# Tanh-shrink feed-forward on one core: opening and steps 0 to 8 written as one list, later weight conversions dealt over other steps

## The chip, the core and the metric

One core of a Trainium2 chip runs the whole program as one launch. The metric is the device time of that launch in microseconds; lower is better. The engines have names here as in the profile: PE (TensorE), DVE (VectorE), ACT (ScalarE), POOL (GpSimd), SP (the queue that issues the DMAs).

## What is computed

Three stages in a row on 2176 tokens of width 512: banded attention with global tokens, a soft mixture of experts with 32 slots, and a feed-forward with a tanh-shrink. Only the end of the second stage and the third matter here:

```python
    return (c @ slot_out).astype(np.float32)   # end of _moe_ref, c is the softmax over 32 slots
...
def _moe2_ref(x, w_in, w_out) -> np.ndarray:
    h = x @ w_in
    g = h - np.tanh(h)
    return (g @ w_out).astype(np.float32)
```

w_in is 512 x 2048 and w_out 2048 x 512, both in float64 in memory.

## The kernel before

**What the feed-forward does.** The kernel never forms x. It folds the slot outputs into w_in: M = slot_out @ w_in has 32 rows, and h = c @ M. M is made in five blocks of columns (`BLOCKS`: 128, 384 and three of 512). The 17 tiles of 128 tokens are worked in six phases (`PHASES`) of 6, 6 and 5 tiles, each for eight of the 16 chunks of 128 hidden columns; that gives 48 steps, steps 0 to 15 and 24 to 39 with six tiles, 16 to 23 and 40 to 47 with five. The PE accumulates one phase's tiles in six PSUM banks, tile a. At the end of a phase of the first half (steps 7, 15, 23) ACT copies each bank to SBUF (`keep_part`, L1220), and the next phase's first products reuse the bank.

**One step i.** For each of its two parts (three and three tiles, or three and two): the head `g_head`, one product on the PE into a PSUM tile h (L1171; two banks in rotation); `g_square` on ACT (L1178); `g_tail0` and `g_tail1` on DVE (L1184, L1188), which make g = h³(h² - 2.5) (the factor -2/15 stands at the output); `g_hi` on ACT rounds g to the PE's short form (L1195) and `g_lo` on POOL takes the remainder (L1199). `ff` then issues three products of 512 columns for each tile: hi with the weight's hi (L1212), hi with its lo (L1213), lo with its hi (L1214). So a six-tile step has 18 products and two heads. The loop works two steps ahead: in step i the PE does the products of step i and the heads of i + 2 and i + 3, and the tails belong to step i + 2.

**Conversions.** Each chunk of w_out (c = 0 to 15) and of the later half of w_in (c = 24 to 31) must become float32 first. One conversion is an ACT operation on the raw words (`f32_head`, L542), then three on DVE: `shift` (L546, tensor_scalar), `high` (L551) and `low` (L556, both with two SBUF inputs). For w_out come two more: the weight's hi on ACT (L1072) and its lo on POOL (L1073). They go through two buffers k_w. The table `JOBS` gives the step in which a chunk is converted, `MB` the steps in which the fourth and fifth block of M are made. In the step's program order on DVE: first tail, second tail, S (shift), first tail, H (high), second tail, L (low).

**The order.** The scheduler is off (`tc.manual_schedule`); each engine runs its instructions in the order in which the code issues them. The opening, from L1276 to the loop at L1370, is straight code: conversion 0, the sums over slots scaled and turned (sos, sot, soT), blocks 0 to 2 of M (`m_rows` L1121, `m_rows_out` L1130, `m_parts` L1135, `m_hi` L1139, `m_lo` L1143), the heads and tails of steps 0 to 2 and the products of step 0. The loop takes over with step 1.

## Time and profile before

| | us |
|---|---|
| median of 3 runs | 403.71 (402.14 to 404.92) |
| the profiled execution | 403.34 |
| its span in the trace | 401.5 |
| PE busy | 380.0 (95%) |
| DVE busy | 275.1 (69%) |
| ACT busy | 218.2 (54%) |
| POOL busy | 208.5 (52%) |

The feed-forward's share begins at about 173 us of the span, behind the last product of the experts, and lasts to the end. The granted clock of the PE is full (1.00) in every stretch from 172 us to 390 us. A profile's busy time of the PE counts overlapping products with modelled ends; how fast it goes is read from the distance between starts.

### The profile page before, as it was taken

To read this page: it belongs to the slowest core of one execution; us is meant where nothing else is said; L and a number is where in the kernel's file an instruction comes from. 1 tells how busy PE (TensorE), PEld (TensorE's weight loads), DVE (VectorE), ACT (ScalarE), POOL (GpSimd) and SP (SyncE) were. 2 spreads that over 40 slices of the span, in tenths; PEclk is the share of its full clock that TensorE was granted. 3 is DMA by queue.
4 is the path that set the end of the run, shared out by engine and by line. 5 is a ranking of instruction groups with operands and counts; after the bars stand their busy time and mean duration, and the time that the engine had idled before them with its cause. 6 is when DMAs were issued, how large, how long until landed. Compare 5 with 4: busy or idle time off the path is not lost.

```text
span 401.5 us, 10209 instructions
## 1 busy us (share of the span) xinstructions
PE 380.0 (95%) x3767; PEld 281.3 (70%) x3767; DVE 275.1 (69%) x833; ACT 218.2 (54%) x542; POOL 208.5 (52%) x275
## 2 busy tenths in 40 slices
PE   6979989898999899999999999999989999999994
PEld 3768777677888333337877786886868888888873
DVE  3577787776576346359998786697879997555541
ACT  2677876765786103258656645565675554445430
POOL 2667685574673010018866433555565667447441
PEclk8999999999999899999999999999999999999999
DMA  7799999999879999997112101013000003003004
GB/s 181 206 398 322 353 327 306 347 349 306 297 214 291 331 360 418 417 419 284 55 33 73 52 1 54 0 23 122 15 2 2 0 26 132 0 2 123 36 2 139
DMA packets 33978, 70.43 MB, mean 175 GB/s; under 512 B 3840, under 2 KB 10752, under 8 KB 33920
## 3 DMA queue, kind: packets, MB, share of 16 engines
q1 hardware_dynamic: 33776, 69.56, 50.8%
q8 instruction: 32, 0.52, 0.5%
q14 instruction: 26, 0.21, 0.2%
q10 hardware_dynamic: 144, 0.13, 0.1%
HBM read 65.22 MB, written 4.46 MB: 174 GB/s over the span
## 4 chain that ended last, share of the span: by engine, by line
PE 77%; issue 6%; DVE 5%; POOL 5%; ACT 4%; DMA 1%; SPq 0%; DVEq 0%; POOLq 0%; ACTq 0%
PE a L1214 13%; PE a L1212 13%; PE a L1213 13%; PE sc L248 7%; PE a L1007 4%; PE X L281 4%; PE a L1046 4%; PE h L1171 3%; PE ptp L269 3%; PE gsc L441 2%; POOL slot L1199 2%; PE xTp L317 2%; DVE slot L1188 1%; PE xgp L486 1%; POOL q L210 1%
## 5 line engine op out<-in xcount | busy, mean ns | idle before, releaser
L1199 POOL TENSOR_TENSOR slot<-slot 128x384 fp32r<-128x384 f32 x96 | 98.6, 1031 | 83.5 <-ACT slot L1195 81.6
L1212 PE MATMUL a<-slot 128*128 128x512 f32 x272 | 107.1, 394 | 1.3 <-ACT v_w L1220 0.7
L1214 PE MATMUL a<-slot 128*128 128x512 f32 x272 | 107.7, 396 | 0.0
L1213 PE MATMUL a<-slot 128*128 128x512 f32 x272 | 107.3, 394 | 0.0
L1184 DVE SCALAR_TENSOR_TENSOR h<-slot,h 128x384 f32<-128x384 f32 x96 | 51.6, 537 | 39.4 <-ACT slot L1178 39.1
L1195 ACT CAST slot<-slot 128x384 fp32r<-128x384 f32 x96 | 47.7, 497 | 49.0 <-DVE slot L1188 48.5
L1178 ACT ACTIVATE slot<-h 128x384 f32<-128x384 f32 x96 | 45.4, 474 | 34.7 <-PE h L1171 34.2
L1212 PEld LDWEIGHTS a<-slot 128*128 128x128 f32 x272 | 51.1, 188 | 13.9 <-ACT v_w L1220 1.5
L1214 PEld LDWEIGHTS a<-slot 128*128 128x128 f32 x272 | 51.0, 188 | 11.5
L1213 PEld LDWEIGHTS a<-slot 128*128 128x128 f32 x272 | 51.1, 188 | 9.2 <-POOL slot L1073 1.1
L1188 DVE TENSOR_TENSOR slot<-slot,h 128x384 f32<-128x384 f32 x96 | 50.8, 530 | 7.3
L258 ACT ACTIVATE sm<-sm,mb 128x128 f32<-128x128 f32 x128 | 41.3, 397 | 17.4 <-DVE mb L254 17.1
L248 PE MATMUL sc<-k,q 128*64 128x128 f32 x512 | 40.3, 299 | 5.1 <-ACT q L216 2.6
L210 POOL TENSOR_SCALAR v<-v 32x1300 f32<-32x1300 f32 (+5 forms) x40 | 33.3, 833 | 15.9 <-PE xgp L486 12.8
L248 PEld LDWEIGHTS sc<-k,q 128*64 128x64 f32 x512 | 34.2, 208 | 9.3 <-issue 5.4
L210 POOL TENSOR_SCALAR q<-q 64x256 f32<-64x256 f32 x62 | 27.7, 447 | 19.2 <-issue 7.7
L1073 POOL TENSOR_TENSOR slot<-k_w,slot 128x512 fp32r<-128x512 f32 x16 | 20.8, 1297 | 31.8 <-ACT slot L1072 31.8
L254 DVE CUSTOM_DVE_ANT_0 sm<-sc,mask 128x128 f32<-128x128 f32 x128 | 29.9, 284 | 5.1 <-PE sc L248 4.6
L1171 PE MATMUL h<-slot 128*128 128x384 f32 x96 | 32.5, 341 | 0.9 <-DVE slot L1188 0.6
L1171 PEld LDWEIGHTS h<-slot 128*128 128x128 f32 x96 | 17.9, 187 | 12.1 <-DVE slot L1188 5.9
L281 PE MATMUL X<-v,pt 128*32 128x65 f32 x1024 | 23.4, 223 | 2.3 <-issue 2.2
L281 PEld LDWEIGHTS X<-v,pt 128*32 128x32 f32 x1024 | 17.1, 109 | 8.4 <-issue 7.4
(245 smaller groups left out, 528.2 us busy)
## 6 DMA issues: line engine op xcount, KB each, us to landing
slot<-in_w_dram SPq DMA_DIRECT2D x54, 512.0 KB, 7.3
slot<-in_w_out_dram SPq DMA_DIRECT2D x9, 512.0 KB, 3.7
slot<-in_w_in_dram SPq DMA_DIRECT2D x16, 256.0 KB, 6.9
k<-in_k_dram SPq DMA_DIRECT2D x7, 576.0 KB, 7.5
q<-in_q_dram SPq DMA_DIRECT2D x15, 256.0 KB, 5.4
out_dram<-o SPq DMA_DIRECT2D x15, 256.0 KB, 2.2
slot<-in_w_in_dram SPq DMA_DIRECT2D x7, 512.0 KB, 9.8
v<-in_v_dram SPq DMA_DIRECT2D x8, 390.0 KB, 5.1
```

Of the source, the lines that this page charges most:

```text
L210: G.tensor_scalar(out=o, in0=i, scalar1=0.0, scalar2=1.0, op0=ALU.add, op1=ALU.mult)
L248: T.matmul(sc[64 * i:64 * i + 64, a, :], lhsT=q_b[2][:, 256 * i + jj:256 * i + 256:4], rhs=k[:, i, :, WINDOWS[t][jj][0]], skip_group_check ...
L281: T.matmul(X[32 * jj:32 * jj + 32, h, :], lhsT=pt[:, 128 * jj + 32 * h:128 * jj + 32 * h + 32], rhs=v[:, WINDOWS[t][jj][0], 65 * h:65 * h ...
L1171: T.matmul(h, lhsT=mst(128 * fc, 128), rhs=cst(128 * t0 + c.start, n))
L1178: S.activation(out=u, in_=h, func=AF.Square)
L1184: V.scalar_tensor_tensor(out=h, in0=u, scalar=-2.5, in1=h, op0=ALU.add, op1=ALU.mult)
L1188: V.tensor_tensor(out=g, in0=u, in1=h, op=ALU.mult)
L1195: S.copy(out=ghi, in_=g)
L1199: G.tensor_tensor(out=glo, in0=g, in1=ghi.bitcast(F32), op=ALU.subtract)
L1212: T.matmul(acc_t[j], lhsT=ghi[:, c], rhs=whi[fc], start=first, stop=False)
L1213: T.matmul(acc_t[j], lhsT=ghi[:, c], rhs=wlo[fc], start=False, stop=False)
L1214: T.matmul(acc_t[j], lhsT=glo[:, c], rhs=whi[fc], start=False, stop=last)
```

## The change

**One list.** The straight code of the opening and the loop's steps 1 to 8 are replaced by `OPENING`, a string of 274 words; each word is one operation with its step, part or chunk (`t0:5:1` is the first tail of step 5, part 1; `T:2:3` the three products of tile 3 of step 2; `S:4`, `H:4`, `L:4` the DVE operations of chunk 4, `head:4` its ACT operation; `h`, `sq`, `hi`, `lo` as above; `keep:2` the copy of bank 2). The loop starts at step 9. With the list come four edits of the opening: the scaling of the sums is cut into an ACT half and a DVE half; the turn multiplies by a four-fold selector (`irep_m`), so that its result can be used by block 0 of M as an ordinary product of full width, which needs no copy and no second product; block 1's copy goes to DVE; part 0 of step 0 is cut into 128 and 256 columns (parts 2 and 3). The two products that only kept the PE busy (`keep_warm`, 512 and 256 columns) become one of 256.

**The later conversions.** Chunk 28 moves from step 13 to 12, 30 and 31 from 16 and 17 to 15 and 16, chunks 8, 9 and 10 from 19, 20, 22 to 18, 19, 21, chunk 12 from 25 to 24; block 3 of M from step 13 to 14. `AHEAD`, which paces the loads, goes from 5 to 4.

```diff
-EARLY, AHEAD = 8, 5
+EARLY, AHEAD = 8, 4
 JOBS = {
-    1: 3, 2: 4, 3: 5, 4: 6, 5: 7, 7: 24, 8: 25, 10: 26, 11: 27, 13: 28, 14: 29, 16: 30, 17: 31,
-    19: 8, 20: 9, 22: 10, 23: 11, 25: 12, 26: 13, 28: 14, 29: 15,
+    1: 3, 2: 4, 3: 5, 4: 6, 5: 7, 7: 24, 8: 25, 10: 26, 11: 27, 12: 28, 14: 29, 15: 30, 16: 31,
+    18: 8, 19: 9, 21: 10, 23: 11, 24: 12, 26: 13, 28: 14, 29: 15,
 }
-MB = {13: 3, 19: 4}
+MB = {14: 3, 19: 4}
+OPENING = """
+    sos:0 sos:1 head:1 S:1 turn:0 turn:1 turn:2 turn:3 soT:0 m0:0 m0:1 soT:1 m0:2 m0:3 head:2 mhi:0 H:1 L:1 whi:1
+    wlo:1 mlo:0 rows:1 ms:1 S:2 h:0:2 sq:0:2 h:0:3 sq:0:3 h:0:1 sq:0:1 t0:0:2 t1:0:2 t0:0:3 t1:0:3 hi:0:2 parts:1
...
+"""
+LOOP = 9
...
+        def sums_copy(k):
+            c = slice(256 * k, 256 * k + 256)
+            if k:
+                V.tensor_scalar(out=sos[:, c], in0=sop[:, c], scalar1=rr, scalar2=None, op0=ALU.mult)
+            else:
+                S.activation(out=sos[:, c], in_=sop[:, c], func=AF.Copy, scale=rr)
...
+        def m_first(k):
+            if k == 0:
+                mp_t[0] = bank(0)[:, 0:128]
+            T.matmul(mp_t[0], lhsT=soT[:, k, :], rhs=win[k][:, 0:128], start=k == 0, stop=k == 3)
...
+        for word in OPENING.split():
+            name, *a = word.split(":")
+            ops[name](*map(int, a))
...
         for i, (t0, nt, fc, first, last) in enumerate(steps):
-            while late and len(free) + len(cool) > 1 and len(LATE) - len(late) < 3 + sum(k < i + AHEAD for k in JOBS):
-                load_late()
-            if i == 0:
+            if i < LOOP:
                 continue
+            late_loads(i)
```

The PE behind the last product of the experts, before: turn (L1289), rows of blocks 0, 1, 2 (L1121), second products (L1135) and the first heads (L1171).

```order
L1289 MATMUL h<-istk,sos 128x32 x4
L1121 MATMUL a_3203<-win_100,mask_93 32x128 x4
L1121 MATMUL a_3208<-win_100,mask_93 32x384 x4
L1121 MATMUL a_3216<-win_101,mask_93 32x512 x4
L1135 MATMUL a_3222<-ms,mask_94 128x128
L1135 MATMUL a_3227<-ms,mask_94 128x384
L1171 MATMUL h<-slot 128x384 x2
L1135 MATMUL a_3244<-ms,mask_94 128x512
L1171 MATMUL h<-slot 128x384
L654 MATMUL a_3252<-win_100,ident 128x256
```

The same place after the change; L1327 is block 0's product of full width, L1355 are the heads of 128 and 256 columns.

```order
L1318 MATMUL h<-mask_94,sos 128x128 x4
L1327 MATMUL a_3207<-win_100,soT 128x128 x4
L1139 MATMUL a_3220<-win_100,soT 32x384 x4
L1355 MATMUL h<-slot 128x128
L1355 MATMUL h<-slot 128x256
L1196 MATMUL h<-slot 128x384
L1153 MATMUL a_3242<-ms,mask_94 128x384
L1139 MATMUL a_3244<-win_101,soT 32x512 x4
L1235 MATMUL a_3250<-slot 128x512
```

One copy and one product are gone between the turn and the first head, the rows of blocks 1 and 2 stand behind block 0, and the first product of step 0 (L1235) stands ahead of the second product of block 2.

DVE at the same place, before: S, H, L of chunk 0, the copy of the turned sums (L1290), S, H, L of chunk 1, the remainders of blocks 0 and 1 (L1143), tails.

```order
L556 SCALAR_TENSOR_TENSOR k_w<-slot,k_w 128x512
L1290 COPY mask_93<-h 128x128
L546 TENSOR_SCALAR k_w<-k_w 128x512
L551 SCALAR_TENSOR_TENSOR k_w<-v_w,k_w 128x512
L556 SCALAR_TENSOR_TENSOR k_w<-v_w,k_w 128x512
L1143 TENSOR_TENSOR slot<-a_3222,slot 64x128
L1143 TENSOR_TENSOR slot<-a_3227,slot 64x384
L1184 SCALAR_TENSOR_TENSOR h<-slot,h 128x384
```

After; L1312 and the two L232 are the work that DVE takes over, the second L565 is S of chunk 2.

```order
L575 SCALAR_TENSOR_TENSOR k_w<-slot,k_w 128x512
L1312 TENSOR_SCALAR sos<-a_2828,mrun 128x256
L565 TENSOR_SCALAR k_w<-k_w 128x512
L232 COPY soT<-h 128x256
L570 SCALAR_TENSOR_TENSOR k_w<-v_w,k_w 128x512
L575 SCALAR_TENSOR_TENSOR k_w<-v_w,k_w 128x512
L1161 TENSOR_TENSOR slot<-a_3207,slot 64x128
L232 COPY ms<-a_3220 128x384
L565 TENSOR_SCALAR k_w<-k_w 128x512
L1206 SCALAR_TENSOR_TENSOR h<-slot,h 128x128
```

S of chunk 1 moves ahead of the copy, three operations on PSUM are added, and S of chunk 2 stands ahead of the first tail.

DVE around the end of the third phase, before: the conversions of chunk 10 (step 22) and chunk 11 (step 23), with the tails of steps 24 and 25 between their operations.

```order
L546 TENSOR_SCALAR k_w<-k_w 128x512
L1184 SCALAR_TENSOR_TENSOR h<-slot,h 128x384
L551 SCALAR_TENSOR_TENSOR k_w<-slot,k_w 128x512
L1188 TENSOR_TENSOR slot<-slot,h 128x384
L556 SCALAR_TENSOR_TENSOR k_w<-slot,k_w 128x512
L1184 SCALAR_TENSOR_TENSOR h<-slot,h 128x384
L1188 TENSOR_TENSOR slot<-slot,h 128x384
L546 TENSOR_SCALAR k_w<-k_w 128x512
L1184 SCALAR_TENSOR_TENSOR h<-slot,h 128x384
L551 SCALAR_TENSOR_TENSOR k_w<-slot,k_w 128x512
```

After, from the last operation of chunk 10 (now step 21) to S of chunk 11 (step 23).

```order
L575 SCALAR_TENSOR_TENSOR k_w<-slot,k_w 128x512
L1206 SCALAR_TENSOR_TENSOR h<-slot,h 128x384
L1210 TENSOR_TENSOR slot<-slot,h 128x384
L1206 SCALAR_TENSOR_TENSOR h<-slot,h 128x384
L1210 TENSOR_TENSOR slot<-slot,h 128x384
L1206 SCALAR_TENSOR_TENSOR h<-slot,h 128x384
L1210 TENSOR_TENSOR slot<-slot,h 128x384
L565 TENSOR_SCALAR k_w<-k_w 128x512
```

Step 22 has no conversion now, so that three pairs of tails stand between the two conversions instead of one; chunk 12 follows in step 24 instead of 25.

## Rows read from the trace of the kernel before

**Rows 1.** Windows; columns: stretch, length, busy us (instructions) of each engine, clock, DMA.
```profile
172.00:178.00 6.00, 5.62 (x53) 2.45 (x42) 2.56 (x5) 2.64 (x6) 1.27 (x1) 1.00 1.03 421
...
194.00:198.00 4.00, 4.00 (x19) 3.24 (x18) 4.00 (x6) 1.99 (x4) 2.54 (x3) 1.00 0.47 131
```
**Rows 2.** Timeline, PE: the first product of steps 0, 1, 8, 9, 15, 16, 23 to 26.
```profile
182.28 0.39 PE L1212 MATMUL a<-slot 128*128 128x512 f32 x1
...
187.08 0.39 PE L1212 MATMUL a<-slot 128*128 128x512 f32 x1
...
220.16 0.50 PE L1212 MATMUL a<-slot 128*128 128x512 f32 x1
...
225.00 0.40 PE L1212 MATMUL a<-slot 128*128 128x512 f32 x1
...
254.69 0.40 PE L1212 MATMUL a<-slot 128*128 128x512 f32 x1
...
259.16 0.39 PE L1212 MATMUL a<-slot 128*128 128x512 f32 x1
...
287.80 0.40 PE L1212 MATMUL a<-slot 128*128 128x512 f32 x1
...
292.77 0.50 PE L1212 MATMUL a<-slot 128*128 128x512 f32 x1 [0.60 <-ACT q L1220]
...
298.38 0.39 PE L1212 MATMUL a<-slot 128*128 128x512 f32 x1
...
302.91 0.40 PE L1212 MATMUL a<-slot 128*128 128x512 f32 x1
```
**Rows 3.** Timeline of the opening; start, duration, engine, line, operation, idle time before.
```profile
173.38 0.69 ACT L1286 ACTIVATE sos<-a,mrun 128x512 f32<-128x512 f32 x1 [0.18 <-PE a L1046]
...
175.24 0.29 DVE L1290 COPY mask<-h 128x128 f32<-128x128 f32 x1 [2.69 <-PE h L1289]
...
176.13 0.27 ACT L1130 COPY ms<-a 128x128 f32<-128x128 f32 x1 [1.51 <-PE a L1121]
...
177.45 1.14 PE L1135 MATMUL a<-ms,mask 128*128 128x128 f32 x4
...
178.27 0.29 DVE L1143 TENSOR_TENSOR slot<-a,slot 64x128 fp32r<-64x128 f32 x1 [0.96 <-DMA slot<-in_w_out_dram]
```
**Rows 4.** Timeline: one square and one tail of 256 columns.
```profile
278.72 0.39 ACT L1178 ACTIVATE slot<-h 128x256 f32<-128x256 f32 x1 [0.66 <-PE h L1171]
...
279.63 0.42 DVE L1184 SCALAR_TENSOR_TENSOR h<-slot,h 128x256 f32<-128x256 f32 x1
```
**Rows 5.** Timeline of step 5: POOL, the conversion on DVE, the head; last row, step 8's tail.
```profile
204.24 1.30 POOL L1073 TENSOR_TENSOR slot<-k_w,slot 128x512 fp32r<-128x512 f32 x1
...
204.75 1.07 DVE L546 TENSOR_SCALAR k_w<-k_w 128x512 int32<-128x512 int32 x1
...
205.50 1.20 POOL L1199 TENSOR_TENSOR slot<-slot 128x384 fp32r<-128x384 f32 x1
...
206.21 1.04 DVE L551 SCALAR_TENSOR_TENSOR k_w<-slot,k_w 128x512 int32<-128x512 int32 x1
...
207.17 0.54 DVE L1188 TENSOR_TENSOR slot<-slot,h 128x384 f32<-128x384 f32 x1
...
207.64 0.68 DVE L556 SCALAR_TENSOR_TENSOR k_w<-slot,k_w 128x512 int32<-128x512 int32 x1
...
207.77 0.44 PE L1171 MATMUL h<-slot 128*128 128x384 f32 x1
...
214.43 0.55 DVE L1188 TENSOR_TENSOR slot<-slot,h 128x384 f32<-128x384 f32 x1
```
**Rows 6.** Timeline at the end of step 23: second tail, rounding, copy of the bank.
```profile
291.12 0.55 DVE L1188 TENSOR_TENSOR slot<-slot,h 128x384 f32<-128x384 f32 x1
...
291.71 0.51 ACT L1195 CAST slot<-slot 128x384 fp32r<-128x384 f32 x1 [0.39 <-DVE slot L1188]
292.13 0.59 ACT L1220 ACTIVATE q<-a 128x512 f32<-128x512 f32 x1
```

More of the change, by code (lines that the diff above doesn't have):

```diff
@@ L1163, in cols, with g_bank @@
             return slice(n, 128 * nt) if part else slice(0, n)
-        def g_head(i, part):
+        def g_bank(i, part):
             nonlocal n_u
-            t0, nt, fc = steps[i][:3]
             c = cols(i, part)
@@ L1170, in g_head @@
             h = hbank()[:, 0:n]
-            T.matmul(h, lhsT=mst(128 * fc, 128), rhs=cst(128 * t0 + c.start, n))
             u, g = (r[:, n_u % 2, 0:n] for r in (u_r, g_r))
@@ L1174, in g_head @@
             u_t[i, part] = h, u, g
+            return c, n
+        def g_head(i, part):
+            t0, nt, fc = steps[i][:3]
+            c, n = g_bank(i, part)
+            T.matmul(u_t[i, part][0], lhsT=mst(128 * fc, 128), rhs=cst(128 * t0 + c.start, n))
         def g_square(i, part):
@@ L1190, in g_parts @@
         def g_parts(i, part):
-            return [u_t[i, part][2]] + [x[:, cols(i, part)] for x in gs_r[i % 3]]
+            c = sub[part] if part > 1 else cols(i, part)
+            return [u_t[i, part][2]] + [x[:, c] for x in gs_r[i % 3]]
         def g_hi(i, part):
@@ L1360, in band_attention_soft_moe_tanhshrink_kernel @@
-        g_head(3, 0)
-        c2[3]()
-        g_tail1(2, 1)
-        g_square(3, 0)
-        c2[4]()
-        c2[5]()
-        g_hi(2, 1)
-        g_lo(2, 1)
+        for f in conv_ops(0):
+            f()
+        keep_warm(bank(0), 256)
+        sos = wk.tile([128, 512], F32, tag="pt", name="sos")
+        rep = wk.tile([128, 512], F32, tag="pt", name="soT")
+        soT = rep.rearrange("p (k s) -> p k s", k=4)
+        sot = hbank()
+        cops, sub = {}, {2: slice(0, 128), 3: slice(128, 384)}
@@ new lines, in m_first, with head, conv @@
+        def m_first(k):
+            if k == 0:
+                mp_t[0] = bank(0)[:, 0:128]
+            T.matmul(mp_t[0], lhsT=soT[:, k, :], rhs=win[k][:, 0:128], start=k == 0, stop=k == 3)
+        def head(c):
+            if c < 16:
+                conv_head(c)
+            else:
+                win_room(c - 16)
+                win_head(c - 16)
+        def conv(k, c):
+            if c not in cops:
+                cops[c] = conv_ops(c) if c < 16 else win_ops(c - 16)
+            cops[c][k]()
@@ new lines, in of_sub, with go, h_sub @@
+        def of_sub(f):
+            def go(i, part):
+                if part < 2:
+                    return f(i, part)
+                t = u_t[i, part] = [x[:, sub[part]] for x in u_t[i, 0]]
+                f(i, part)
+            return go
+        def h_sub(i, part):
+            if part < 2:
+                return g_head(i, part)
+            if part == 2:
+                g_bank(i, 0)
+            c = sub[part]
+            T.matmul(u_t[i, 0][0][:, c], lhsT=mst(128 * steps[i][2], 128), rhs=cst(c.start, c.stop - c.start))
@@ new lines, in products @@
+        def products(i, j):
+            if j == 0:
+                late_loads(i)
+            ff(i, [j])
+        ops = {
+            "sos": sums_copy, "turn": sums_turn, "soT": turned_copy, "m0": m_first, "head": head,
+            "S": lambda c: conv(1, c), "H": lambda c: conv(2, c), "L": lambda c: conv(3, c),
+            "whi": lambda c: conv(4, c), "wlo": lambda c: conv(5, c),
+            "rows": lambda b: m_rows(b, b), "ms": lambda b: m_rows_out(b, vcopy if b == 1 else scopy), "parts": lambda b: m_parts(b, b + 2),
+            "mhi": m_hi, "mlo": m_lo, "h": h_sub, "sq": of_sub(g_square), "t0": of_sub(g_tail0), "t1": of_sub(g_tail1),
+            "hi": of_sub(g_hi), "lo": of_sub(g_lo), "T": products,
+            "keep": lambda j: keep_part(0, j, -2.0 / 15.0),
+        }
@@ L1368, in band_attention_soft_moe_tanhshrink_kernel, with late_loads @@
+        def late_loads(i):
+            while late and len(free) + len(cool) > 1 and len(LATE) - len(late) < 3 + sum(k < i + AHEAD for k in JOBS):
+                load_late()
+        for word in OPENING.split():
+            name, *a = word.split(":")
+            ops[name](*map(int, a))
         es_x.close()
```

112 lines of the change are left out of this document (25 added, 87 removed).

## The prediction

> **What bounds the kernel now.** I read the table by engine first: the PE is busy 95% of the span, so time can only come from places where its products start later than the pace allows. Next the timeline of the PE alone, with the first product of each step looked up (18 products to a six-tile step). The pace is that of an undisturbed step: step 25 lasts 302.91 - 298.38 = 4.53 us; a five-tile step, at five sixths of it, 3.78 us. Against this pace four places lose [rows 2]:
> - The opening. The experts' last product is read at 173.38 [rows 3]; step 0 begins at 182.28 and step 1 at 187.08 [rows 2].
> - Steps 1 to 8: 225.00 - 187.08 = 37.92 us for eight steps, 8 x 4.53 = 36.24 at pace; 1.68 too long.
> - Step 23: 292.77 - 287.80 = 4.97 instead of 3.78, 1.19 too long; step 24: 298.38 - 292.77 = 5.61, 1.08 too long.
> - Step 15, with a phase's end of the same kind behind it, lasts 259.16 - 254.69 = 4.47 and loses nothing, so a phase's end need not cost anything.
>
> Then why. In the opening one chain runs through all engines, and between its links they stand: DVE waits 2.69 us for the turn, ACT 1.51 us for block 0's rows [rows 3], and DVE is busy 2.56 of 6 us; from step 2 on it is busy without a break, 4.00 of 4 us [rows 1]. There the windows name the second bound: DVE with POOL. In step 5 S takes 1.07 us and ends at 205.82, just behind POOL's operation that ends at 204.24 + 1.30 = 205.54; H takes 1.04 and ends at 207.25, behind POOL's at 206.70; the second tail then ends at 207.71, and the next head starts at 207.77 [rows 5]. So the head waits for DVE, and in the PE's fixed order the products behind it wait too, although their operands are there: step 8's first tail ends at 214.98, its first product starts only at 220.16, 5.2 us later [rows 2, 5].
>
> That S and H wait for POOL is also the rule of the Trainium skill, SBUF — State Buffer, section "Who interferes with whom": a DVE operation with two SBUF inputs, or in the two-port mode, and a GpSimd operation that reads SBUF take a shared port pair in turn, and whoever comes second waits out the whole instruction. The ends above agree (0.28 and 0.55 us behind POOL's ends). It speaks against the change: a list that puts S, H and L in a row does not make the port wider. What that would do is the third rival below.
>
> **The opening, part by part.** In units of the rows [rows 3]:
> - Scaling in halves. Before 0.69 us on ACT. A half of 256 columns took 0.39 on ACT and 0.42 on DVE in other operations [rows 4]. In the changed program DVE's half waits for ACT's, so the first half is there 0.3 us earlier and the second at about 0.39 + 0.42 = 0.81, 0.1 later; the first two turns run beneath it. Gain 0 to 0.3; I take 0.1.
> - The wait between the halves has its rule too: the Trainium skill, PSUM — Partial Sum Buffer, section "PSUM bank collisions raise a hardware error", forbids ACT and DVE to read one bank at once. By it the halves can gain nothing side by side; the sum above already has them in turn.
> - Turn and copy. The turn's eight passes stay, with 128 columns instead of 32. No row has this form alone; between nothing and the 1.14 us that four passes of 128 and 384 columns took [rows 3] I take 0.1 more. The copy of 0.29 becomes two of 256, in turn, 0.39 + 0.42, with block 0's first two products beneath the second: 0.5 later.
> - Block 0. Gone from the chain: the copy of 0.27 at 176.13 and its wait, and the second product. Before, from the turned copy's end at 175.53 to block 0's remainder at 178.56 it took 3.03 us. After: two products behind the second copy (0.6, from four passes in 1.14), rounding 0.27, remainder 0.29, and hand-overs of some 0.1: about 1.4. But DVE now has H and L of chunk 1 ahead of that remainder, so that it ends near 177.8 instead of 178.56: gain 0.75.
> - First product. Cutting part 0 lets 128 columns go through square, two tails and rounding in 4 x 0.29 instead of 4 x 0.55: 1.0 less. S of chunk 2 stands in front of the first tail: 0.4, or 1.5 if POOL has begun the weight's lo (1.30) [rows 5]; both become ready within 0.1 us of each other, so I take the middle.
> Step 0 then begins near 179.8 instead of 182.28. It now also contains block 2's second product (about 1.1) and more heads, so step 1 begins near 185.8 instead of 187.08: **1.3 us earlier** (ends: 0.5, with S behind POOL and the copies in full; 1.8).
>
> On DVE little is won: it loses 2 us of waiting, and gets some 1.3 us of new work (the half of the sums, the larger copy, block 1's copy). It reaches step 2's tails about when it did.
>
> **Steps 1 to 8.** Same 10 conversions, same heads, tails and products. What changes is the order: in the list a head stands half a step to a step later among the products (head 7:1 behind three fourths of step 5 instead of its middle, 8:1 at the end of step 6 instead of its middle), so the PE can use up the 5.2 us that it lay behind DVE. It needs only the rounding (0.51) and POOL's remainder (1.20) behind the tail, 2 us with hand-overs, so up to 3 us can be used. All of the 1.68 us can go in this way. DVE bounds it: tails of 4 x 0.55 = 2.2 and a conversion of 1.07 + 1.04 + 0.68 = 2.8 make 5.0 us a step against 4.53 [rows 5]. Since the PE starts 1.3 earlier and DVE does not, five such steps eat 5 x 0.47 = 2.4 of the 3.0. I take **1.2 of 1.68**; ends: -0.8 (no better than before, and half the opening's gain lost at the heads) and 1.68. The copies of the banks stand directly behind the last product of each tile instead of three at a time; they lie beneath products and are in the same figure.
>
> **The later conversions.** At the end of step 23 the chain is: second tail 291.67, rounding to 292.22, behind it on ACT the copy of the bank to 292.72, and the next phase's first product waits 0.60 for it [rows 2, 6]. DVE is late because chunks 10 and 11 are converted in steps 22 and 23, next to each other, where a short step gives 3.78 us and two tails and a conversion ask for 5.0. Now step 22 is free: 3.78 - 2.2 = 1.6 us to catch up, more than the 1.19 that step 23 lost. Chunk 12 in step 24 asks 5.0 of 4.53, 0.5 lost at the most, until the free step 25. So of 1.19 + 1.08 = 2.27 I take back **1.6** (ends 0 and 2.27). Chunks 28, 30, 31, 8, 9 and block 3 move by one step: each still meets one conversion or one block a step, beneath the PE's 4.53; I cost them at nothing, ends -0.6 and +0.4, the size of what one crowded step loses. The loads move with `AHEAD` by one step of 4.53 us, while the DMA share is under a half (0.47) even in step 3 and later lower; nothing.
>
> **Sum.** 1.3 + 1.2 + 1.6 = 4.1 us. From the profiled execution's own 403.34 (span 401.5 and 1.8 around it) that is 399.2; the median of the runs is 0.4 higher, so 399.6 as a median.
>
> **The rivals.**
> - The PE keeps pace everywhere: 1.8 + 1.68 + 2.27 = 5.75, 398.0. For it: DVE's waits in the old order are largely hand-overs that another order can avoid, and step 15 shows a free phase's end. Against: 5.0 us of DVE work a step.
> - Given back at the heads: DVE, no earlier than before, stops the PE at the first heads, and step 9 begins only 0.5 us earlier. Then 403.7 - 0.5 - 1.6 = 401.6. For it: DVE 4.00 of 4 busy. Against: the 5.2 us of lag.
> - Slower, by the port. The list has S, H and L of chunks 5, 6, 7 in a row; where POOL has a backlog, L waits too: 1.20 + 0.55 instead of 0.68 is 1.07 more a conversion, 8.6 us for eight. The lag covers 3.0, 5.6 are lost, 4.1 won: 403.7 + 1.5 = 405.2. It decides from 7.1 us of additional DVE waiting. For it: POOL has 1.30 + 2 x 1.20 a step, and its port time and DVE's together, 3.7 + 0.28 + 2 x 0.55 = 5.1, exceed 4.53. Against: before, S and H already wait like this, and only L is free.
>
> **How the numbers follow.** A measurement of this kernel can tell about 1%, 4 us, from no change. Forecast 0.50, of which 0.28 lies below 399.67; all on pace 0.20; given back at the heads 0.20; slower by the port 0.10, half of it beyond 407.7. Faster by over 1%: 0.28 + 0.20 = 0.48; slower by over 1%: 0.05; the rest, 0.47, within 1%. The range from 397.2 to 403.6 leaves out about 0.08 on either side.
>
> **What would show it.** In the new profile: step 1's first product near 185.8 and step 9's near 222.5; the distance between first products 4.53 in steps 5 to 7 too; no wait for the bank's copy at the end of step 23. If step 1 begins early and step 9 does not, the heads' waits for the second tail show it, and the second rival holds. If DVE's H and L grow beyond 1.04 and 0.68 on average, the third does. The forecast is wrong if step 9 begins before 221 or after 224.5, or if steps 23 and 24 still take over 10 us together.

## The result and the profile after

| us | before | after |
|---|---|---|
| median of 11 runs each, same chip | 403.45 (400.81 to 404.92) | 398.69 (396.81 to 401.52) |
| the profiled execution | 403.34 | 396.81 |
| its span | 401.5 | 395.0 |
| PE busy | 380.0 | 375.8 |
| DVE, POOL busy | 275.1, 208.5 | 272.9, 210.2 |

The ratio after to before is 0.9916, with a 95% interval of 0.9889 to 0.9942: 2.3 to 4.5 us less. The change made the kernel faster, by about 0.8%.

The two spans differ by 6.5 us, more than the change did. The product that keeps the PE busy stands directly behind the last product of the experts in both kernels; up to there they run the same operations. It starts at 173.24 us before, and at 169.82 after: 3.42 us of the difference lie ahead of the change. From the start of the feed-forward's last product to the end of the span the kernel after takes 0.48 us longer (6.31 against 5.83); in the fourteen profiled executions this last stretch takes between 5.74 and 6.58 us. Between these two points 3.58 us were won: 3.42 + 3.58 - 0.48 = 6.52.

The timeline of the PE in the kernel before, the product that keeps it busy:

```profile
173.24 1.13 PE L654 MATMUL a<-win,ident 128*128 128x512 f32 x2
```

The same view of the kernel after: this product, and the first products of steps 0, 1, 9, 15 and 23 to 26, as in [rows 2].

```profile
169.82 0.70 PE L673 MATMUL a<-win,ident 128*128 128x256 f32 x2
...
177.12 0.50 PE L1235 MATMUL a<-slot 128*128 128x512 f32 x1
...
183.54 0.39 PE L1235 MATMUL a<-slot 128*128 128x512 f32 x1
...
219.78 0.39 PE L1235 MATMUL a<-slot 128*128 128x512 f32 x1
...
249.11 0.40 PE L1235 MATMUL a<-slot 128*128 128x512 f32 x1
...
282.08 0.40 PE L1235 MATMUL a<-slot 128*128 128x512 f32 x1
...
286.56 0.50 PE L1235 MATMUL a<-slot 128*128 128x512 f32 x1 [0.52 <-ACT q L1243]
...
291.40 0.39 PE L1235 MATMUL a<-slot 128*128 128x512 f32 x1
...
295.93 0.40 PE L1235 MATMUL a<-slot 128*128 128x512 f32 x1
```

From here on every time called **relative** is counted from the start of that product, so that what lies ahead of the change drops out. Each comes from one profiled execution. With the first product of each step in both timelines:

| relative us | before | after | won in this stretch |
|---|---|---|---|
| first product of step 0 | 9.04 | 7.30 | 1.74 |
| of step 1 | 13.84 | 13.72 | -1.62 (0.12 in all) |
| of step 9 | 51.76 | 49.96 | 1.68 |
| of step 10 | 56.29 | 54.66 | -0.17 |
| of step 15 | 81.45 | 79.29 | 0.53 (block 3) |
| of step 23 | 114.56 | 112.26 | 0.14 |
| of step 25 | 125.14 | 121.58 | 1.26 |
| last product | 222.42 | 218.84 | 0.02 |

The sum is 3.58 us. So the opening as such gave nothing, steps 1 to 8 together run exactly at pace (49.96 - 13.72 = 36.24 = 8 x 4.53; single steps last from 4.09 to 4.84, since their heads lie unevenly), step 9 gives back 0.17, where a head waits for DVE's second tail, and the later conversions gave more than the two steps at the phase's end.

Windows of the kernel after, columns as in [rows 1], over the same clock times (the work in them is 3.4 us further on):

```profile
172.00:178.00 6.00, 5.30 (x32) 2.56 (x32) 5.58 (x11) 3.86 (x11) 1.73 (x2) 1.00 1.03 423
...
194.00:198.00 4.00, 4.00 (x20) 3.25 (x18) 3.67 (x7) 3.01 (x6) 3.79 (x4) 1.00 0.00 0
```

In the opening DVE is now busy 5.58 of 6 us, and from 194 us on it has time left (3.67 of 4), where it had none before.

The timeline of the opening after: block 0's remainder (DVE L1161), POOL's weight lo (L1091), S of chunk 2 (L565), the first tail (L1206), the rows of block 2 on the PE (L1139), block 1's remainder (the second L1161), the head behind it, and block 2's second product.

```profile
173.94 0.29 DVE L1161 TENSOR_TENSOR slot<-a,slot 64x128 fp32r<-64x128 f32 x1
...
174.64 1.27 POOL L1091 TENSOR_TENSOR slot<-k_w,slot 128x512 fp32r<-128x512 f32 x1 [3.49 <-ACT slot L1090]
174.85 1.34 DVE L565 TENSOR_SCALAR k_w<-k_w 128x512 int32<-128x512 int32 x1
...
176.12 0.28 DVE L1206 SCALAR_TENSOR_TENSOR h<-slot,h 128x128 f32<-128x128 f32 x1
176.12 1.07 PE L1139 MATMUL a<-win,soT 128*32 128x512 f32 x8
...
177.67 0.56 DVE L1161 TENSOR_TENSOR slot<-a,slot 64x384 fp32r<-64x384 f32 x1
...
178.28 0.44 PE L1196 MATMUL h<-slot 128*128 128x384 f32 x1
178.56 1.02 PE L1153 MATMUL a<-ms,mask 128*128 128x512 f32 x2
```

S waits out POOL's operation (it ends at 176.19, POOL's at 175.91). The first product of step 0, at 177.12, follows on the PE's rows of block 2; a head behind it waits for block 1's remainder, which ends at 178.23, and block 2's second product (L1153) comes within step 0.

Groups of instructions on DVE from step 0 to step 8, before (182 to 225 us: S, then H) and after (175 to 222 us: S, L, H); columns: count, busy us, mean ns, idle time ahead. These groups hold six of the eight S, and three of the H and of the L; the others stand in groups with other tiles.

```profile
L546 DVE TENSOR_SCALAR k_w<-k_w 128x512 int32<-128x512 int32 x6 | 5.9, 985 | 0.0
...
L551 DVE SCALAR_TENSOR_TENSOR k_w<-slot,k_w 128x512 int32<-128x512 int32 x3 | 3.1, 1039 | 0.0
```

```profile
L565 DVE TENSOR_SCALAR k_w<-k_w 128x512 int32<-128x512 int32 x6 | 3.7, 613 | 0.0
L575 DVE SCALAR_TENSOR_TENSOR k_w<-slot,k_w 128x512 int32<-128x512 int32 x3 | 2.4, 807 | 0.1
L570 DVE SCALAR_TENSOR_TENSOR k_w<-slot,k_w 128x512 int32<-128x512 int32 x3 | 2.2, 726 | 0.1
```

In these groups S fell from 985 to 613 ns (one of the six after is the opening's S of 1.34 us) and H from 1039 to 726; L (L575) rose from 678 ns before to 807, so some of the waiting for POOL has moved to it. Over all of S, H and L in these stretches the three means add up to 2.7 us a conversion before and 2.2 after.

The end of step 23 after, the counterpart of [rows 6]: rounding, the first operation of chunk 12 (L561), POOL's remainder, H of chunk 11 (L570), the copy of the bank (L1243), the second tail.

```profile
284.96 0.51 ACT L1218 CAST slot<-slot 128x384 fp32r<-128x384 f32 x1
...
285.36 0.66 ACT L561 ACTIVATE k_w<-slot 128x512 f32<-128x512 f32 x1
285.54 1.00 POOL L1222 TENSOR_TENSOR slot<-slot 128x384 fp32r<-128x384 f32 x1 [1.38 <-ACT slot L1218]
285.56 1.53 DVE L570 SCALAR_TENSOR_TENSOR k_w<-slot,k_w 128x512 int32<-128x512 int32 x1
...
285.92 0.58 ACT L1243 ACTIVATE q<-a 128x512 f32<-128x512 f32 x1
...
287.01 0.54 DVE L1210 TENSOR_TENSOR slot<-slot,h 128x384 f32<-128x384 f32 x1
```

Ahead of the copy there stands an operation that was not there before, and the next phase's first product still waits 0.52 us for the copy. H takes 1.53 us beside POOL's remainder.

### The profile page after: what moved, and what is told of

It reads as the page before. It is cut to its first block, busy times and chain, and to the rows that moved or that the text cites. A ratio compares the mean times of both kernels' runs of the same rounds, so it can differ in the third digit from the quotient of the medians.

```text
span 395.0 us, 10198 instructions
## 1 busy us (share of the span) xinstructions
PE 375.8 (95%) x3764; PEld 281.8 (71%) x3764; DVE 272.9 (69%) x837; ACT 218.2 (55%) x543; POOL 210.2 (53%) x276
## 4 chain that ended last, share of the span: by engine, by line
## 5 line engine op out<-in xcount | busy, mean ns | idle before, releaser
L1222 POOL TENSOR_TENSOR slot<-slot 128x384 fp32r<-128x384 f32 (+2 forms) x97 | 100.2, 1037 | 80.2 <-ACT slot L1218 76.6
L1235 PE MATMUL a<-slot 128*128 128x512 f32 x272 | 107.4, 395 | 0.5 <-ACT q L1243 0.5
L1206 DVE SCALAR_TENSOR_TENSOR h<-slot,h 128x384 f32<-128x384 f32 (+2 forms) x97 | 51.6, 533 | 38.4 <-ACT slot L1200 38.1
L1218 ACT CAST slot<-slot 128x384 fp32r<-128x384 f32 (+2 forms) x97 | 47.6, 492 | 39.5 <-DVE slot L1210 38.2
L1200 ACT ACTIVATE slot<-h 128x384 f32<-128x384 f32 (+2 forms) x97 | 45.2, 470 | 40.3 <-PE h L1196 39.3
L1235 PEld LDWEIGHTS a<-slot 128*128 128x128 f32 x272 | 51.1, 188 | 13.9 <-ACT q L1243 0.9
L1210 DVE TENSOR_TENSOR slot<-slot,h 128x384 f32<-128x384 f32 (+2 forms) x97 | 51.0, 526 | 8.2 <-DVE h L1206 0.5
L1091 POOL TENSOR_TENSOR slot<-k_w,slot 128x512 fp32r<-128x512 f32 x16 | 20.9, 1308 | 29.6 <-ACT slot L1090 29.3
L1196 PE MATMUL h<-slot 128*128 128x384 f32 (+1 forms) x95 | 31.3, 338 | 0.1
L300 PE MATMUL X<-v,pt 128*32 128x65 f32 x1024 | 22.4, 223 | 2.0 <-issue 2.0
```

Source lines behind the costliest of these rows:

```text
L1196: T.matmul(u_t[i, part][0], lhsT=mst(128 * fc, 128), rhs=cst(128 * t0 + c.start, n))
L1200: S.activation(out=u, in_=h, func=AF.Square)
L1206: V.scalar_tensor_tensor(out=h, in0=u, scalar=-2.5, in1=h, op0=ALU.add, op1=ALU.mult)
L1210: V.tensor_tensor(out=g, in0=u, in1=h, op=ALU.mult)
L1218: S.copy(out=ghi, in_=g)
L1222: G.tensor_tensor(out=glo, in0=g, in1=ghi.bitcast(F32), op=ALU.subtract)
```

## The experiments

**The two parts alone.** `list_alone` is the kernel after with the old tables of conversions; `jobs_alone4` is the kernel before with the new tables.

```diff
 # list_alone, from the kernel after
-    1: 3, 2: 4, 3: 5, 4: 6, 5: 7, 7: 24, 8: 25, 10: 26, 11: 27, 12: 28, 14: 29, 15: 30, 16: 31,
-    18: 8, 19: 9, 21: 10, 23: 11, 24: 12, 26: 13, 28: 14, 29: 15,
+    1: 3, 2: 4, 3: 5, 4: 6, 5: 7, 7: 24, 8: 25, 10: 26, 11: 27, 13: 28, 14: 29, 16: 30, 17: 31,
+    19: 8, 20: 9, 22: 10, 23: 11, 25: 12, 26: 13, 28: 14, 29: 15,
-MB = {14: 3, 19: 4}
+MB = {13: 3, 19: 4}
 # jobs_alone4, from the kernel before: the reverse of these lines, and
-EARLY, AHEAD = 8, 5
+EARLY, AHEAD = 8, 4
```

> The changed kernel with JOBS and MB of the kernel before, so only the list of the opening and steps 0 to 8 is new. Measured within the profile from the start of the product that keeps the PE busy (the last product of the experts has just ended) to the start of the last product of the feed-forward: 222.42 us before, 218.84 after. Theory (the two halves act in different places and add up): step 9 begins 49.9 to 50.1 us behind that product as in the changed kernel, steps 23 and 24 lose 2 us again, the stretch is 220.4 to 220.8, the ratio to before 0.995 to 0.997. Rival (the later steps recover because the list leaves DVE ahead): steps 23 and 24 lose no more than 1.2 us together, stretch near 219.

> The kernel before with the new JOBS, MB and AHEAD alone, the opening and steps 0 to 8 untouched. All times from the start of the product that keeps the PE busy. The list alone took 1.51 us off the stretch to the last product (222.42 to 220.91) and gave nothing back later. Theory (both parts add up): step 9 at 51.7 to 51.9, stretch 220.2 to 220.5, that is 2.0 to 2.2 less than before; ratio 0.994 to 0.997. Rival (the later steps need the list's lead): stretch 221.5 or more.

| | ratio to before (95%) | median us | step 1 rel. | step 9 rel. | steps 23 + 24 | last product rel. |
|---|---|---|---|---|---|---|
| before | 1 | | 13.84 | 51.76 | 10.58 | 222.42 |
| list_alone | 0.9977 (0.9944 to 1.001) | 401.62 against 402.05 | 13.73 | 50.05 | 10.59 | 220.91 |
| jobs_alone4 | 0.995 (0.9921 to 0.998) | 401.17 against 403.1 | 13.83 | 51.72 | 9.33 | 220.43 |
| after | 0.9916 (0.9889 to 0.9942) | 398.69 against 403.45 | 13.72 | 49.96 | 9.32 | 218.84 |

The parts add: 1.51 of the list and 1.99 of the tables make 3.50, and both together won 3.58. Neither takes from the other. (`AHEAD` is 4 in both; the new tables with its old value gave no kernel to measure.) This rests on the timelines: by the time alone `list_alone` can't be told from the kernel before, and its stretch, 220.91, lies just above the 220.8 that was expected. The crowded step of block 3 (step 13 before, 14 after) belongs to the tables: 7.14 us in the list alone, 6.49 in the tables alone. Either step converts a chunk beside making block 3; in the new tables the step ahead of it, 13, is free of a conversion, as step 22 is.

**What the 1.68 us of steps 1 to 8 were.** The weight loads of the PE (PEld) show where it stood in the kernel before: in step 5 its second product waits for POOL's lo of the weight, and the head for the second tail; in step 8 a product waits for a bank's copy.

```profile
205.59 0.19 PEld L1213 LDWEIGHTS a<-slot 128*128 128x128 f32 x1 [0.38 <-POOL slot L1073]
...
207.77 0.19 PEld L1171 LDWEIGHTS h<-slot 128*128 128x128 f32 x1 [0.52 <-DVE slot L1188]
...
222.64 0.19 PEld L1212 LDWEIGHTS a<-slot 128*128 128x128 f32 x1 [0.37 <-ACT v_w L1220]
```

The loads run ahead of the products, so a product loses less than its load waits. The first of these waits comes in steps 5, 6 and 7 (0.38, 0.37, 0.38), the second in steps 5 and 6 alone (0.52, 0.49). Step 7, which has only the first, is 0.27 us too long, steps 5 and 6 are 0.55 each and step 8 is 0.31. So, as an estimate from these lengths, about 0.8 of the 1.68 us is the PE waiting for the weight's lo itself, 0.56 the heads and 0.31 step 8 with its copies. The prediction named the heads alone.

`before_pool_fill` is the kernel before; its remainders on POOL (of the weights and of the activations) are filled with zeros instead of computed, so that POOL reads nothing there.

```diff
-                lambda: G.tensor_tensor(out=wlo[c], in0=wf, in1=r[:, 0, :], op=ALU.subtract),
+                lambda: G.memset(r[:, 1, :], 0.0),
...
-            G.tensor_tensor(out=glo, in0=g, in1=ghi.bitcast(F32), op=ALU.subtract)
+            G.memset(glo.bitcast(F32), 0.0)
```

> The kernel before with POOL's two subtractions (the remainders of g and of w_out) replaced by a fill with zeros, so that POOL reads nothing; the products with the remainders then add zeros. The order of every engine stays. Theory A (the old order is slow in steps 5 to 8 because S, H and L wait for POOL's operations, the tail is late and the head behind it stops the PE): S, H and L fall to about 0.42 (or a little more), 0.69 and 0.69, and steps 5 to 8 go at 4.53 instead of 5.08, 5.08, 4.80, 4.84. Theory B (the place of the heads among the products and the two banks are to blame, DVE's speed is not): steps 5 to 8 stay near 5 us.

Groups on DVE in steps 0 to 8 of this run: S, H and L.

```profile
L546 DVE TENSOR_SCALAR k_w<-k_w 128x512 int32<-128x512 int32 x6 | 2.5, 419 | 0.0
L551 DVE SCALAR_TENSOR_TENSOR k_w<-slot,k_w 128x512 int32<-128x512 int32 x3 | 2.1, 685 | 0.0
L556 DVE SCALAR_TENSOR_TENSOR k_w<-slot,k_w 128x512 int32<-128x512 int32 x3 | 2.1, 685 | 0.0
```

S, H and L have their bare durations, 0.42, 0.69 and 0.69 us, a conversion takes 1.8, and steps 5 to 8 run in 4.53, 4.53, 4.54 and 4.58 us instead of 5.08, 5.08, 4.80 and 4.84. Step 13 falls from 7.14 to 6.58, step 23 from 4.97 to 4.06, step 24 from 5.61 to 4.64; step 1 begins at 13.83 as before. So nearly all that steps 1 to 8, 23 and 24 lost [rows 2] goes when POOL's operations no longer read: 1.62 of 1.68 us, 0.91 of 1.19 and 0.97 of 1.08. That a DVE operation with two SBUF inputs waits for a GpSimd operation that reads SBUF, and not for one that only writes, is the rule of the Trainium skill, SBUF — State Buffer, section "Who interferes with whom"; the durations of H and L agree with it, with fills running beside eight of the sixteen here. The fill is also shorter than the subtraction (0.47 us on average for 384 columns) and waits for no rounding, so the weight's lo comes earlier for both reasons, and this run alone doesn't part DVE's waits from POOL's own lateness; `high_behind_tail` below, where POOL's subtractions stay, does so at one place.

**Whether the heads' later places matter.** `heads_earlier` is the kernel after with heads 8:1, 9:1 and 10:0 back at the places that the loop gave them.

```diff
-    ... wlo:6 T:6:2 T:6:0 T:6:4 T:6:1 T:6:5 hi:7:0 lo:7:0 h:8:1 head:25
+    ... wlo:6 T:6:2 T:6:0 T:6:4 hi:7:0 lo:7:0 h:8:1 T:6:1 T:6:5 head:25
...
-    ... S:24 H:24 T:7:0 keep:0 T:7:1 keep:1 T:7:5 T:8:2 t1:8:1 hi:8:1 lo:8:1 h:9:1 sq:9:1 t0:9:1 h:10:0 T:8:1
+    ... S:24 H:24 t1:8:1 hi:8:1 lo:8:1 h:9:1 sq:9:1 t0:9:1 T:7:0 keep:0 T:7:1 keep:1 T:7:5 h:10:0 T:8:2 T:8:1
```

> The changed kernel with heads 8:1 and 9:1 and 10:0 put back to where the kernel before has them among the products (behind three products' tiles of steps 6 and 7, and at the end of step 7). Theory B (later heads let the PE use up its lag): each of these heads waits for its tail, steps 6 to 8 together lose 0.8 to 1.5 us. Theory A (DVE runs without waits for POOL, the heads' place hardly matters): steps 6 to 8 lose under 0.4 us together against the changed kernel's 13.49 (from 206.29 to 219.78).

Timeline of this run in step 7, DVE and PE: S of chunk 25, the second tail behind it, and head 9:1, which waits for that tail.

```profile
220.26 0.48 DVE L565 TENSOR_SCALAR pg<-pg 128x512 int32<-128x512 int32 x1
220.66 0.54 DVE L1210 TENSOR_TENSOR slot<-slot,h 128x384 f32<-128x384 f32 x1
...
221.25 0.44 PE L1196 MATMUL h<-slot 128*128 128x384 f32 x1 [0.73 <-DVE slot L1210]
```

Step 7 takes 5.49 us instead of 4.09, step 9 begins at 51.33 instead of 49.96, and the last product comes 1.33 us later than after. The head stops the PE for 0.73 us, until a tail behind S has ended. So a head's place among the products matters as well as the conversions' places on DVE.

**What is left at the end of step 23.** Four kernels. `chunk10_back` puts chunk 10 back into step 22 (`21: 10` becomes `22: 10`). `head_behind_copy` issues chunk 12's first ACT operation behind the copies of the banks.

```diff
 # head_behind_copy: in part 1, ahead of it
+                if part and parts(i + 3) > 1:
+                    g_head(i + 3, 0)
+                    g_square(i + 3, 0)
+                if last and i < len(steps) - 1:
+                    for j in tiles:
+                        (emit_out if fc == 15 else keep_part)(t0, j, -2.0 / 15.0)
                 if part == 0:
                     c = JOBS.get(i + 1)
...
```

> The changed kernel with chunk 10 back in step 22, next to chunk 11 in step 23; chunk 12 stays in step 24. Theory (conversions in neighbouring steps ahead of the phase's end make the loss): steps 22 to 24 lose 0.8 to 1.5 us more than in the changed kernel (13.12 us there), stretch 219.6 to 220.3 instead of 218.84. Rival (the phase's end loses by ACT's copies alone, wherever chunk 10 is): under 0.3 us more.

> The changed kernel with one edit in the loop: ACT's operation of the next step's conversion is issued behind the copies of the banks instead of ahead of them. In the changed kernel chunk 12's operation (0.66 us on ACT) stands ahead of the first bank's copy at the end of step 23, and the next phase's first product waits 0.52 us. Theory: step 23 lasts 3.8 to 4.0 instead of 4.48, stretch 218.2 to 218.5. Rival (the copy is late because of the rounding and the tail before it): step 23 stays above 4.3.

`chunk10_back`: step 23 takes 5.83 and step 24 6.20 us, the last product comes at 221.58, 2.74 later than after. Its timeline at the end of step 23: S of chunk 11, the copy, and the product that waits for it.

```profile
287.99 1.06 DVE L565 TENSOR_SCALAR k_w<-k_w 128x512 int32<-128x512 int32 x1
...
289.38 0.59 ACT L1243 ACTIVATE q<-a 128x512 f32<-128x512 f32 x1
...
290.02 0.50 PE L1235 MATMUL a<-slot 128*128 128x512 f32 x1 [1.45 <-ACT q L1243]
```

With chunks 10, 11 and 12 in three steps in a row the wait for the copy grows from 0.52 to 1.45 us. The free step 22 is what pays: with chunk 12 in step 24, steps 22 to 24 take 15.82 us without it and 13.12 with it, 2.70 apart, where 0.8 to 1.5 had been expected.

`head_behind_copy`: step 23 falls to 3.93, but step 24 rises to 5.41; the last product comes at 218.94, no earlier than after, where the theory had 218.2 to 218.5. Was chunk 12 then late? `head_ahead` tells: it issues the same operation at the beginning of the phase's last step instead.

```diff
+            if last:
+                next_head(i)
             for part, tiles in enumerate((order[:half], order[half:])):
...
-                if part == 0:
-                    c = JOBS.get(i + 1)
...
+                if part == 0 and not last:
+                    next_head(i)
```

> After with one edit of the loop: in a step that ends a phase, the ACT operation that opens the next step's conversion (chunk 31 in step 15, chunk 12 in step 23) is issued at the step's beginning instead of behind the rounding of part 0, so that it no longer stands ahead of the copy of the bank. In after it takes 0.66 us (285.36 to 286.02) directly ahead of the copy, for which the next phase's first product waits 0.52. After has step 23 in 4.48, step 24 in 4.84, last product at 218.84 behind the start of the product that keeps the PE busy. Theory (this operation's place on ACT is what is left of step 23's loss, and an earlier place keeps chunk 12 on time): step 23 in 3.9 to 4.1, step 24 in 4.7 to 4.9, last product at 218.2 to 218.5, the time 0.4 to 0.6 below after, too little to be seen in the time itself. Rival (as when the operation was put behind the copy, the loss moves on): step 23 in 3.9 to 4.1 but step 24 in 5.2 or more, last product at 218.8 or later.

The rival held: step 23 in 3.94, step 24 in 5.39, last product at 218.96. The time is 400.1 us against 403.11, ratio 0.993 (0.9899 to 0.9962). A late chunk 12 was not the cause, and the next kernel tries what else is late in that place: `high_behind_tail`, as `head_ahead`, and in step 23 H stands behind the second tail.

```diff
+                    k = 2 * part + (i != 23 or part == 0)
                     g_tail0(i + 2, part)
-                    for f in ops[2 * part:2 * part + 1]:
+                    for f in ops[2 * part:k]:
                         f()
                     g_tail1(i + 2, part)
-                    for f in ops[2 * part + 1:2 * part + 2]:
+                    for f in ops[k:2 * part + 2]:
                         f()
```

> As head_ahead, and in step 23 alone H of chunk 11 stands behind the second tail of part 1 instead of ahead of it. In head_ahead H runs there for 1.53 us (289.11 to 290.64) beside POOL's remainder (289.08 to 290.09), the second tail behind it ends at 291.11, and step 24 takes 5.39. Theory (what holds step 24 back is this tail, late by H's wait for POOL): the tail ends 1.2 to 1.5 us earlier against the first product of step 23, step 23 stays at 3.9 to 4.0, step 24 falls to 4.5 to 4.8, last product at 218.0 to 218.4 behind the start of the product that keeps the PE busy (after 218.84, head_ahead 218.96), the time 0.4 to 0.9 below after, at the edge of what five rounds can tell. Rival (DVE is simply full in steps 23 and 24, so that H's and L's new place delays step 26's tails as much): step 24 at 5.2 or more, or the loss appears in step 25; last product at 218.8 or later.

H and the second tail on DVE, and the product of step 24 that waits for a bank's copy, timeline of `head_ahead`:

```profile
289.11 1.53 DVE L570 SCALAR_TENSOR_TENSOR k_w<-slot,k_w 128x512 int32<-128x512 int32 x1
...
290.57 0.54 DVE L1210 TENSOR_TENSOR slot<-slot,h 128x384 f32<-128x384 f32 x1
...
292.59 0.50 PE L1235 MATMUL a<-slot 128*128 128x512 f32 x1 [0.49 <-ACT v_w L1243]
```

The late tail reaches the PE through ACT: the rounding behind it starts at 291.14, and the copy of the fourth bank stands behind the rounding, from 291.94.

The two DVE operations in `high_behind_tail`:

```profile
288.00 0.56 DVE L1210 TENSOR_TENSOR slot<-slot,h 128x384 f32<-128x384 f32 x1
...
288.47 0.86 DVE L570 SCALAR_TENSOR_TENSOR k_w<-slot,k_w 128x512 int32<-128x512 int32 x1
```

Counted from step 23's first product (285.62 and 284.31) the tail ends 4.25 us behind it instead of 5.49; H waits only 0.17 us. Step 24 falls to 4.63, step 23 stays at 3.94, and the last product comes at 218.18, 0.66 earlier than after. What had held step 24 back was the tail behind an H that waits for POOL: `after_pool_fill` below, which leaves H ahead of the tail and takes away its wait, has step 24 in 4.64 too. H's new place in the kernel after, without the edit of `head_ahead`, was not run. The time is 399.59 us against 403.11, ratio 0.9903 (0.9864 to 0.9941). In the timeline it is the shortest of the kernels that compute everything; in the time itself it can't be told from the kernel after (0.9889 to 0.9942).

**Why the opening gave nothing.** Four kernels. `s2_later` moves `S:2` of the list behind `t1:0:3`; `part0_uncut` has part 0 of step 0 in one piece; `part0_uncut_s2` has both; `after_pool_fill` is the kernel after with the two fills shown above.

```diff
 # s2_later
-    ... ms:1 S:2 h:0:2 sq:0:2 h:0:3 sq:0:3 h:0:1 sq:0:1 t0:0:2 t1:0:2 t0:0:3 t1:0:3 hi:0:2 parts:1
+    ... ms:1 h:0:2 sq:0:2 h:0:3 sq:0:3 h:0:1 sq:0:1 t0:0:2 t1:0:2 t0:0:3 t1:0:3 S:2 hi:0:2 parts:1
 # part0_uncut
-    ... ms:1 S:2 h:0:2 sq:0:2 h:0:3 sq:0:3 h:0:1 sq:0:1 t0:0:2 t1:0:2 t0:0:3 t1:0:3 hi:0:2 parts:1
-    rows:2 lo:0:2 T:0:0 ... t1:0:1 hi:0:3 lo:0:3 T:0:2
+    ... ms:1 S:2 h:0:0 sq:0:0 h:0:1 sq:0:1 t0:0:0 t1:0:0 hi:0:0 parts:1
+    rows:2 lo:0:0 T:0:0 ... t1:0:1 T:0:2
```

> The changed kernel with one word of the list moved: S of chunk 2 from ahead of the first tails to behind the four tails of the cut part. There it waited for POOL's remainder of chunk 1 and took 1.34 us instead of 0.42, with every tail queued behind it. Theory: S falls to 0.42 to 0.7, step 1 begins 0.4 to 0.9 us earlier than 13.72, and the stretch is shorter by as much if steps 1 to 8 keep their pace. Rival (DVE's order from then on is the bound): step 1 earlier, step 9 no earlier than 49.8.

> After with part 0 of step 0 as one piece of 384 columns in the list (one head, square, pair of tails, rounding and remainder in place of two of each). Times are from the start of the product that keeps the PE busy; after has its first product of step 0 at 7.30, step 1 at 13.72, step 9 at 49.96. Theory (the prediction's term: the cut spares 4 x 0.55 - 4 x 0.29 = 1.0 us): first product at 8.2 to 8.4; step 1 at 14.2 or later. Rival (the two pieces share one bank, so the second piece's head and square delay the first tail and most of the gain is eaten there): first product at 7.0 to 7.6, step 1 within 0.2 of 13.72.

> As part0_uncut, and S of chunk 2 behind the two tails of part 0 instead of ahead of them. Same clock as there. If S waiting for POOL (1.34 us instead of 0.42) stands ahead of the tails of the uncut part with nothing else beside it: first product 0.7 to 1.0 earlier than in part0_uncut, step 1 0.3 or more earlier. If other work lies beside S here too: first product and step 1 within 0.2 of part0_uncut.

> After with the two remainder subtractions of the loop and the list on POOL (the weight's lo, the activation's lo) replaced by fills with zero of the same shape, so POOL reads nothing there; the low parts are left out of the result. Same clock; after has steps 1 to 8 in 36.24, step 23 4.48, step 24 4.84, last product at 218.84. Theory (the list already puts S, H and L where they do not wait for POOL long enough to reach the PE): steps 1 to 8 within 0.2 of 36.24; steps 23 and 24, which the loop still orders, fall to 4.06 and 4.64 as in the kernel before with the same fill, last product at 218.1 to 218.4. Rival (the port still costs PE time in the list, and the end of step 8 only hides it): steps 1 to 8 in 35.6 or less, last product below 217.8. In the opening, if S of chunk 2 is on the path: first product at 6.4 to 6.6; if not: 7.2 to 7.35.

| relative us | first product of step 0 | of step 1 | of step 9 | last product |
|---|---|---|---|---|
| after | 7.30 | 13.72 | 49.96 | 218.84 |
| s2_later | 7.26 | 13.76 | 50.09 | 218.99 |
| part0_uncut | 8.02 | 14.57 | 50.92 | 219.67 |
| part0_uncut_s2 | 7.22 | 13.77 | 50.09 | 218.78 |
| after_pool_fill | 7.30 | 13.32 | 49.52 | 218.10 |

Timeline of `s2_later`: ACT's squares of the second piece of part 0 and of part 1 (one row for both), the first tail behind them, the rows of block 2 on the PE, the rounding of the first piece, and the first product.

```profile
178.37 0.77 ACT L1200 ACTIVATE slot<-h 128x256 f32<-128x256 f32 x2 [0.47 <-PE h L1355]
178.78 0.30 DVE L1206 SCALAR_TENSOR_TENSOR h<-slot,h 128x128 f32<-128x128 f32 x1 [1.00 <-ACT slot L1200]
...
179.08 1.06 PE L1139 MATMUL a<-win,soT 128*32 128x512 f32 x8
...
179.43 0.30 ACT L1218 CAST slot<-slot 128x128 fp32r<-128x128 f32 x1 [0.30 <-DVE slot L1210]
...
180.07 0.50 PE L1235 MATMUL a<-slot 128*128 128x512 f32 x1
```

S no longer waits (0.42 us), and the first product does not come earlier. Two things lay beside its wait. The two pieces of part 0 share a bank, so the first piece's tail comes only behind the second piece's square (DVE stands idle for 1.00 us); and the PE is busy with the second product of block 1 and the rows of block 2, which the list puts ahead of step 0's first product. Here the rounding ends at 179.73, but the first product starts only at 180.07, when those rows are through. In the kernel after they run from 175.38 to 177.12 without a break, and the rounding ends at 177.05, so that there the chain and the PE's order end almost together.

Timeline of `part0_uncut`: S of chunk 2, the tail of the whole part, the first product.

```profile
178.63 1.34 DVE L565 TENSOR_SCALAR k_w<-k_w 128x512 int32<-128x512 int32 x1
...
179.89 0.55 DVE L1206 SCALAR_TENSOR_TENSOR h<-slot,h 128x384 f32<-128x384 f32 x1
...
181.62 0.50 PE L1235 MATMUL a<-slot 128*128 128x512 f32 x1 [1.06 <-ACT slot L1218]
```

Here S's wait is on the path: moving S away wins 0.80 us at the first product and at step 1. So the cut (0.72 and 0.85 us) and the later S are two cures for the same loss, and together they win no more than either.

How much idle time of the PE was there to win? The windows from the start of the product that keeps it busy to the first product of step 1, before and after, columns as in [rows 1]:

```profile
173.24:187.08 13.84, 12.66 (x72) 7.43 (x68) 10.02 (x20) 9.61 (x21) 6.90 (x6) 1.00 0.96 393
...
169.82:183.54 13.72, 12.59 (x68) 7.82 (x64) 11.69 (x23) 9.65 (x22) 6.16 (x7) 1.00 1.02 417
```

The PE stands idle for 1.18 us before and 1.13 after, as far as modelled ends tell it. The shorter chain took away next to none of this, and although the products that only keep the PE busy have 512 columns less, its busy time stays: other work has taken their place.

`after_pool_fill` shows the rest: the first product stays at 7.30, but step 0 is 0.40 shorter, mostly because block 1's remainder on DVE comes 0.3 us earlier and with it the head that stood in step 0's products. Its step 23 stays at 4.49, against the theory's 4.06, since ACT's order is left there; step 24 falls to 4.64.

## Why the prediction was right, and where it was not

The median, 398.69, is 0.9 us below the forecast of 399.6, and by the trace 3.58 us were won against 4.1 forecast. The terms, however, came out so:

| term | forecast | measured |
|---|---|---|
| opening (step 1 earlier) | 1.3 (0.5 to 1.8) | 0.12 |
| steps 1 to 8 | 1.2 of 1.68 (-0.8 to 1.68) | 1.68 |
| steps 23 and 24 | 1.6 of 2.27 (0 to 2.27) | 1.26 |
| moved chunks, block 3, loads | 0 (-0.6 to 0.4) | 0.53 + 0.14 - 0.17 + 0.02 = 0.52 |
| sum | 4.1 | 3.58 |

Two terms lie outside their own ends, one on each side, so the sum was partly luck.

- **The opening.** The chain to block 0's remainder was sized well: 0.75 forecast, and 5.32 to 4.41 relative, 0.91, measured. "Step 0 then begins near 179.8", 2.5 us earlier, did not follow from the parts, which give 0.75 + 1.0 - 0.95 = 0.8; measured 1.74. The step that failed is that the first product waits only for the chain of square, tails and rounding: the PE's own order puts block 1's second product and block 2's rows ahead of it, and in `s2_later` these hold it back for some 0.3 us after the rounding has ended. The PE's own work was not in the sum at all; its idle time up to step 1 stayed at 1.1 to 1.2 us. Then "it now also contains block 2's second product (about 1.1) and more heads": step 0 grew by 1.62 us instead of 1.2: the product took 1.02 and one head more 0.28, and a head waits for block 1's remainder. What the first product won, step 0 gave back, most of it as PE work that had stood ahead of step 0 before. S of chunk 2 behind POOL came as priced (1.34 us), but at another place: at most some 0.3 to 0.4 us within step 0, by `after_pool_fill`.
- **Steps 1 to 8.** "All of the 1.68 us can go in this way" was right, and "DVE bounds it: ... 5.0 us a step against 4.53" was wrong. That sum took S and H with their waits for POOL as fixed, while the list's places for S, H and L avoid part of them (S 0.99 to 0.61 us, H 1.04 to 0.73 in the groups above): with 2.2 us for a conversion and 2.2 for the tails DVE asks for 4.4 us a step, less than 4.53. The reading of the loss was half right too: the PE waited for the heads, but by the estimate above longer in all for POOL's lo of the weight, for which the sum had no term; in the list that wait is down to 0.17 us at a weight load, and a product is late by 0.05. The heads' later place is needed too, as `heads_earlier` shows, but I had misread one: head 7:1 stands behind two tiles of step 5, not behind three fourths of it; 8:1 stands two tiles later than before, 9:1 four, and several heads stand where they stood or earlier.
- **Steps 23 and 24.** The free step 22 pays (`chunk10_back`). "No wait for the bank's copy at the end of step 23" failed: 0.52 us of it are left. I had costed chunk 12 in step 24 on DVE alone; its first operation stands on ACT ahead of the copy, and H of chunk 11 behind POOL delays the tail that step 24 needs. Both were in reach, and `high_behind_tail` takes them back.
- **Moved chunks.** "I cost them at nothing" was wrong: block 3 in step 14 instead of step 13 shortens the crowded step from 7.14 to 6.50 us. The term rests on "each still meets one conversion or one block a step", which misreads the tables: step 13 had both before, and step 14 has both after; what changed is the free step ahead of it.
- **Rivals.** "Slower, by the port" fell: S, H and L in a row do not wait more, a conversion's S and H wait less. "Given back at the heads" fell, since step 9 begins 1.80 us earlier relative. "The PE keeps pace everywhere" held for steps 1 to 8 only.
- **The marks.** They were set in the clock of the old trace, and the new one reaches the feed-forward 3.42 us earlier. As it stands, step 9 at 219.78 lies below the mark of 221 that would make the forecast wrong; with 3.42 added it begins at 223.20, against 222.5 forecast, and step 1 at 186.96, against 185.8. Steps 23 and 24 take 9.32 us, below the mark of 10. Of the other marks, L's mean did grow beyond 0.68 (0.81), while H's fell: one of the two alone would have misled.
